# Score and value steps of an attention and MLP kernel gathered into three visits per batch

## The chip, the cores and the metric

The kernel runs on one core of one Trainium2 chip. The metric is the device time of one execution in microseconds (us); the time of the kernel before is the median of three runs. All durations in this document are in us where no other unit stands.

## The reference

Two operators follow each other. The first is causal attention with a window of 64 positions, for 8 batches, 8 heads, 576 positions and a head dimension of 64. The second is a layer norm without bias and an MLP with a ReLU and a residual, on the attention's output with the heads side by side (512 features, 2048 hidden).

```python
scores = scale * np.matmul(q, k.transpose(0, 1, 3, 2))
rel = pos[:, None] - pos[None, :]
mask = (rel >= 0) & (rel < window)                 # window = 64
attn = softmax(np.where(mask, scores, -1e9))
x = np.matmul(attn, v)                             # heads side by side: (8, 576, 512)
xn = (x - mu) / np.sqrt(var + 1e-06) * g_ln
out = x + np.maximum(xn @ w_ch1, 0.0) @ w_ch2      # (512, 2048), (2048, 512)
```

## The kernel before

Work is cut into nine groups. Group g from 0 to 7 is the first 512 positions of batch g; group 8 is the last 64 positions of all eight batches, as four blocks ("tails", one for two batches each). A group has four blocks of 128 rows.

The attention of one block has two steps on TensorE. The score step `s_mm(g, j)` makes 16 small matmuls (64 rows deep, 64 columns wide) into two PSUM banks of the pool `ps_s` (tag "sc"), lets ScalarE take the exp of both banks into an f16 tile `pt`, and `s_mask` multiplies `pt` with the window mask on VectorE. The value step `b_step(g, kb)` makes 16 matmuls (128 deep, 64 stationary columns) of `pt` with the values into the two banks of `ps_x` (tag "xps"); then VectorE makes the rows of the block: reciprocal of the sums, multiplication, mean and variance. `z_step` normalizes these rows on GpSimd, and `zt_step` transposes them, for batches from 2 on by a DMA from SP's queue (block 3 of batches 3 and 5 on TensorE). So the score matmuls, the value matmuls and the full 128x128 matmuls of the MLP are three kinds that use the array in different shapes.

The MLP of a group is a list of units. From group 2 on there are 30: 16 units `l1(hc)`, four matmuls of 512 columns each and a ReLU on ScalarE, with two PSUM banks in turn; then 14 units `stage(n, p)`, two for each of the seven products of a Strassen-like second layer, in the order 1, 2, 6, 5, 7, 4, 3. Three banks A, B and C collect these products. Between products VectorE adds a bank to the residual rows (`post`, line 485), while later products go on accumulating into the same bank: bank A is read after product 1 and then written by product 6. `s_sums` makes sums of the hidden activations on VectorE that the products need.

The MLP of group g and the attention of batch b = g + 1 run together. The order on every engine is written out by hand: `at(i, f, ...)` puts a call into slot i, and after unit i the calls of slot i are made, in the order in which they were put there. The instructions of one engine run in the order of these calls, and the framework puts semaphore waits where a tile is read or reused. Each tile tag has a fixed number of buffers: `ps_s` has two banks, "xps" one tile of two banks, `ps_t` the banks t0 and t1 (for transposes on TensorE and for bank C), `pt` four buffers.

In groups 2 to 6 the value step of block j and the score step of block j+1 share slots 2, 7 and 12; the value step of block 3 stands in slot 17, and the score step of block 0 of the batch after next in slot 27 of the group before (slot 31 of group 1 for batch 3):

```python
            for j in range(4):
                if j:
                    at((2, 7, 12)[j - 1], s_mm, b, j)
                    at((3, 8, 13)[j - 1], s_mask, b, j)
                at((2, 7, 12, 17)[j], b_step, b, j)
                at((2, 7, 12, 17)[j], z_step, b, j)
```

Groups 3 and 5 also carry one tail block each, with its score step in slot 1 and its value step in slot 5. Group 2 carries in addition four `w2_sums` on VectorE (slots 4 to 7). For batches from 4 on, GpSimd casts q and k to f16 in four casts (`cast_qk`, line 128), three in slot 11 and one in slot 16; the q halves are then transposed by DMAs from SP's queue (slot 13) and the k halves on TensorE (slots 17 and 21; 18 and 22 in group 2). The loads of q and k are issued at the end of the group before.

Of the kernel before, what the change touches and what calls it, by code (L numbers as in the profile page):

```python
# [10 lines left out]
FP32 = mybir.dt.float32  # L11
# [4 lines left out]
ALU = mybir.AluOpType  # L16
# [4 lines left out]
def kernel(  # L21
# [10 lines left out]
    nc = tc.nc  # L32
    B, H, S, D = q.shape
# [3 lines left out]
    NGRP = B + 1  # L37
    NKC = DM // 128
    NHC = HID // 128
    NHP = H // 2  # L40
    EPS = 1e-6
    XQ = 3
# [13 lines left out]
    ps_s = ctx.enter_context(tc.tile_pool(name="pss", bufs=2, space=PSUM))  # L56
    ps_x = ctx.enter_context(tc.tile_pool(name="psx", bufs=1, space=PSUM))
# [22 lines left out]
    tail32, tail16, tailT, vT = {}, {}, {}, {}  # L80
# [157 lines left out]
    def t_tail(i, x):  # L238
# [19 lines left out]
        evac(0, tailT[i][x], tp)  # L258

    def s_mm(g, j, pe_mask=False):  # L260
        sc = [ps_s.tile([128, NHP, 2, 64], FP32, tag="sc", name=f"sc_{g}_{j}_{par}") for par in range(2)]
        pt = p_pt.tile([128, 2, NHP, 2, 64], FP16, tag="pt", name=f"pt_{g}_{j}")
        pts[(g, j)] = pt
        if pe_mask:
            m = mbias[:, :]
            mb = bass.AP(tensor=m.tensor, offset=m.offset, ap=[m.ap[0], [0, NHP * 2], m.ap[1]])
            for par in range(2):
                nc.tensor.matmul(
                    out=sc[par][:, :].rearrange("p h w i -> p (h w) i"), lhsT=ident16, rhs=mb,
                    start=True, stop=False, skip_group_check=True,  # L270
                )
# [16 lines left out]

        for par in range(2):
            o, i = pt[:, par], sc[par][:, :]  # L290
            if XQ <= g < NGRP - 1:
                o = o.rearrange("p h w (r j) -> p (h w) r j", j=4)
                i = i.rearrange("p h w (j r) -> p (h w) r j", j=4)
            nc.scalar.activation(out=o, in_=i, func=AF.Exp, bias=0.0, scale=scale)  # L294
# [7 lines left out]

    def b_step(g, kb):
        kblk = f"{g}_{kb}"
        sfx, nb = ("r", 2) if g == NGRP - 1 else ("", None)
# [5 lines left out]
        xn = xv.rearrange("p (h d) -> p h d", h=H)  # L311
        xps = ps_x.tile([128, H, 128], FP32, tag="xps", name=f"xps_{kblk}")
        pt = pts.pop((g, kb))
        for h in range(H):
            par, hp = h % 2, h // 2
            for r in range(2):
                if sfx:
                    rhs = vT[kb][:, r, h, :]
                else:
                    rhs = (vA if r else vB)[g][:, kb, h, :]  # L320
                nc.tensor.matmul(out=xps[64 * r:64 * r + 64, h, :D + 1], lhsT=pt[:, par, hp, r, :], rhs=rhs,  # L321
                                 start=True, stop=True)
        rcp = p_blk.tile([128, H], FP32, tag="rcp", name=f"rcp_{kblk}")
        nc.vector.reciprocal(out=rcp, in_=xps[:, :, D])  # L324
        rcp_b = bass.AP(tensor=rcp.tensor, offset=rcp[:, :].offset,
                        ap=[rcp[:, :].ap[0], rcp[:, :].ap[1], [0, D]])
        nc.vector.tensor_tensor(out=xn, in0=xps[:, :, 0:D], in1=rcp_b, op=ALU.mult)  # L327
        stats = p_blk.tile([128, nc.vector.BN_STATS_DIM], FP32, tag="stats", name=f"stats_{kblk}")
# [512 lines left out]
    for g in range(NGRP):  # L841
# [7 lines left out]
        def at(i, f, *a):  # L849
            slots[min(i, len(slots) - 1)].append((f, a))  # L850

        b = g + 1
        if g == 0:
# [29 lines left out]
        if g == 1:  # L883
# [35 lines left out]
            at(17, make_vB, 3)  # L919
            at(31, s_mm, 3, 0)  # L920
            at(31, s_mask, 3, 0)
            for i, (x, half) in zip((12, 24, 12, 28), ((0, 0), (1, 0), (0, 1), (1, 1))):
# [8 lines left out]
        if g > 1 and g + 2 < B:  # L931
            at(11, alloc_qkT, g + 2)
            if g + 2 >= XQ:
                at(11, cast_qk, g + 2, 0, (0,))
                at(11, cast_qk, g + 2, 1, (0,))
                at(11, cast_qk, g + 2, 0, (1,))
            else:
                at(11, cast_qk, g + 2, 0)
        if g > 1 and b < B:
            for j in range(4):  # L940
                if j:
                    at((2, 7, 12)[j - 1], s_mm, b, j)
                    at((3, 8, 13)[j - 1], s_mask, b, j)
                at((2, 7, 12, 17)[j], b_step, b, j)
                at((2, 7, 12, 17)[j], z_step, b, j)
                at((12, 12, 18, {3: 24, 5: 23}.get(b, 22))[j], zt_step, b, j)
        for n, i in enumerate(TAILS.get(g, ())):
            ts = (13, 13, 17, 22) if n else (1, 2, 5, 11)
            at(ts[0], s_mm, NGRP - 1, i)
            at(ts[1], s_mask, NGRP - 1, i)  # L950
            at(ts[2], b_step, NGRP - 1, i)
            at(ts[2], z_step, NGRP - 1, i)
            at(ts[3], zt_step, NGRP - 1, i)
        n = g + 2
        if g > 1 and n < B:
            at(16, cast_qk, n, 1, (1,) if n >= XQ else (0, 1))
            at(20, alloc_v, n)
# [4 lines left out]
            for i, (x, half) in zip((13, 18, 13, 22) if g == 2 else (13, 17, 13, 21),  # L962
                                    ((0, 0), (1, 0), (0, 1), (1, 1))):
                at(i, t_main, n, x, half, 0)
            at(27, s_mm, n, 0)
            at(28, s_mask, n, 0)
            if n + 1 < B:
# [64 lines left out]
```

## Time and profile before

| what | value |
|---|---|
| runs of the kernel before | 310.21, 308.94, 310.77; median 310.21 us |
| profiled execution, span from first to last instruction | 305.9 us |
| profiled execution, own time | not given beside the span |
| TensorE, share of the span | 97% (295.4 us) |
| VectorE, GpSimd, ScalarE | 72%, 57%, 49% |
| granted clock of TensorE, mean | 0.995 of full speed |
| groups 2, 3, 4, 5, 6, length on TensorE | 31.37, 31.30, 31.36, 31.29, 29.04 us |

In the rows of a timeline the first number is the start in us from the beginning of the span and the second the duration in us; then come the engine, the line of the kernel, the operation, the tile written and the tiles read, the shapes, and the number of instructions merged into the row. In square brackets stands the idle time of the engine before the row and what ended it. Matmuls are pipelined, so a duration contains latency, and the time that a matmul takes up is read from start to start. PE is TensorE, DVE VectorE, ACT ScalarE, POOL GpSimd, SP the queue that issues most DMAs.

Groups start (first `hps` matmul) at 92.50 (group 2), 123.87 (3), 155.17 (4), 186.53 (5), 217.82 (6) and 246.86 (7).

### The profile page before, as it was taken

How to read it: one execution, taken by the hardware profiler on the slowest of the kernel's cores; microseconds unless marked ns; L12 is line 12 of the kernel's file. 1: busy time of each engine (PE TensorE's matmuls, PEld its weight loads, DVE VectorE, ACT ScalarE, POOL GpSimd, SP SyncE). 2: the span in 40 equal slices, each digit the busy share in tenths (PEclk: the TensorE clock that was granted, in tenths of full speed). 3: DMA queues.
4: the chain of work that ended last, by engine and by line, in shares of the span. 5: the costliest groups of instructions: out<-in, count | busy, mean ns of one | idle time of the engine just before them, and what ended most of it. 6: DMA issues, size and time to landing. Idle time of an engine off the chain costs nothing.

```text
span 305.9 us, 7582 instructions
## 1 busy us (share of the span) xinstructions
PE 295.4 (97%) x3061; PEld 196.4 (64%) x3061; DVE 220.6 (72%) x412; ACT 150.7 (49%) x253; POOL 173.3 (57%) x256
## 2 busy tenths in 40 slices
PE   6989999999999999999999999999999999999992
PEld 4557545687454478547854786469646854788882
DVE  0778696767766995589656965896669685789972
ACT  2586635587227733775157527752475046306500
POOL 7589676564952789179806983698146507014300
PEclk9999999999999999999999999999999999999998
DMA  8999999999776997899189997993790399003014
GB/s 191 266 385 301 314 366 286 303 284 236 150 181 228 243 172 147 280 280 127 35 243 303 204 160 245 298 155 70 215 175 19 53 189 208 19 17 139 0 38 103
DMA packets 113669, 58.35 MB, mean 191 GB/s; under 512 B 83617, under 2 KB 104609, under 8 KB 113634
## 3 DMA queue, kind: packets, MB, share of 16 engines
q1 hardware_dynamic: 112576, 54.67, 74.0%
q0 software_dynamic: 768, 2.80, 3.8%
q8 instruction: 24, 0.39, 0.5%
q10 hardware_dynamic: 290, 0.40, 0.5%
q14 instruction: 11, 0.09, 0.1%
HBM read 38.80 MB, written 9.44 MB: 158 GB/s over the span
## 4 chain that ended last, share of the span: by engine, by line
PE 89%; SPq 4%; DMA 2%; POOL 1%; ACT 1%; DVE 1%; issue 0%; ACTq 0%
PE hps L401 30%; PE pA L478 12%; PE pB L478 8%; PE pC L478 8%; PE hph L537 6%; PE ch L413 6%; PE xps L321 4%; PE sc L286 4%; PE ch L554 3%; PE tp L229 3%; PE lA L592 2%; DMA w1s<-in_moe_w_ch_dram 2%; SPq L141 2%; POOL w1g L190 1%; SPq L89 1%; PE lC L592 1%
## 5 line engine op out<-in xcount | busy, mean ns | idle before, releaser
L401 PE MATMUL hps<-zT,w1g 128*128 128x512 f16 x416 | 95.3, 380 | 0.0
L405 ACT ACTIVATE hrT<-hps 128x512 f16<-128x512 f32 x104 | 62.3, 599 | 39.3 <-PE hps L401 35.7
L401 PEld LDWEIGHTS <-w1g 128*128 128x128 f16 x416 | 38.6, 98 | 43.3 <-issue 0.7
L294 ACT ACTIVATE pt<-sc 128x512 f16<-128x512 f32 x72 | 39.0, 594 | 27.7 <-PE sc L286 20.5
L478 PEld LDWEIGHTS <-sS 128*128 128x128 f16 x448 | 43.4, 98 | 4.9
L351 POOL TENSOR_SCALAR rsz<-mvg 128x1 f32<-128x1 f32 x28 | 10.2, 364 | 60.6 <-DVE mvg L332 59.8
L128 POOL CAST qk<-qk 128x1024 f16<-128x1024 f32 x32 | 36.3, 1147 | 11.3 <-DMA qk<-in_k_dram 5.6
L478 PEld LDWEIGHTS <-hrT 128*128 128x128 f16 x336 | 32.4, 98 | 5.5 <-ACT hrT L637 0.3
L301 DVE TENSOR_TENSOR pt<-pt,mask 128x1024 f16<-128x1024 f16 x32 | 27.5, 867 | 8.4 <-ACT pt L294 8.4
L215 ACT COPY qkT<-tp 128x1024 f16<-128x1024 f16 x16 | 16.1, 1012 | 34.1 <-PE tp L229 34.1
L485 DVE TENSOR_TENSOR xn<-pA,xn 128x512 f32<-128x512 f32 x28 | 19.2, 685 | 16.7 <-PE pA L478 11.1
L478 PE MATMUL pC<-w2s,sS 128*128 128x256 f16 x224 | 27.1, 273 | 0.0
L478 PE MATMUL pA<-wT,sS 128*128 128x256 f16 x224 | 26.9, 273 | 0.0
L354 POOL TENSOR_SCALAR z<-xn,rsz 128x512 f16<-128x512 f32 x28 | 24.9, 888 | 2.9
L327 DVE TENSOR_TENSOR xn<-xps,rcp 128x512 f32<-128x512 f32 x36 | 24.9, 691 | 1.5 <-DMA out_dram<-xn 0.3
L329 DVE BATCH_NORM_STATS2 stats<-xn 128x6 f32<-128x512 f32 x36 | 25.0, 695 | 1.2
L324 DVE RECIPROCAL rcp<-xps 128x8 f32<-128x8 f32 x36 | 7.3, 204 | 24.7 <-PE xps L321 24.7
L452 DVE TENSOR_TENSOR sS<-hrT 128x512 f16<-128x512 f16 (+1 forms) x40 | 24.5, 613 | 0.6 <-ACT hrT L405 0.6
L537 PE MATMUL hph<-zT,w1g 128*128 128x256 f16 x192 | 23.8, 273 | 1.0 <-DVE zT L371 0.5
L321 PEld LDWEIGHTS <-pt 128*64 128x64 f16 x576 | 12.2, 110 | 13.7 <-issue 5.5
L352 POOL TENSOR_TENSOR rsz<-rsz,mhalf 128x1 f32<-128x1 f32 x28 | 19.4, 692 | 2.3
L147 POOL CAST vA<-v 128x1024 f16<-128x1024 f32 (+2 forms) x19 | 17.4, 930 | 5.6 <-DMA v<-in_v_dram 5.6
(113 smaller groups left out, 448.9 us busy)
## 6 DMA issues: line engine op xcount, KB each, us to landing
out_dram<-xn SPq DMA_DIRECT2D x33, 256.0 KB, 2.8
qk<-in_q_dram SPq DMA_DIRECT2D x16, 512.0 KB, 6.2
qk<-in_k_dram SPq DMA_DIRECT2D x16, 512.0 KB, 6.9
v<-in_v_dram SPq DMA_DIRECT2D x32, 256.0 KB, 7.7
w2s<-in_moe_w_ch_dram SPq DMA_DIRECT2D x9, 512.0 KB, 9.2
w1s<-in_moe_w_ch_dram SPq DMA_DIRECT2D x4, 512.0 KB, 7.3
tk<-in_k_dram SPq DMA_DIRECT2D x8, 256.0 KB, 4.5
tv<-in_v_dram SPq DMA_DIRECT2D x8, 256.0 KB, 5.0
```

Of the source, the lines that this page charges most:

```text
L128: nc.gpsimd.tensor_copy(out=dst[:, :].rearrange("p (a j) e d -> p a e j d", j=j), in_=t[:, :].rearrange("p (a e j d) -> p a e j d", e=2, j ...
L294: nc.scalar.activation(out=o, in_=i, func=AF.Exp, bias=0.0, scale=scale)
L301: nc.vector.tensor_tensor(out=ptv, in0=ptv, in1=mb, op=ALU.mult)
L321: nc.tensor.matmul(out=xps[64 * r:64 * r + 64, h, :D + 1], lhsT=pt[:, par, hp, r, :], rhs=rhs, start=True, stop=True)
L327: nc.vector.tensor_tensor(out=xn, in0=xps[:, :, 0:D], in1=rcp_b, op=ALU.mult)
L329: nc.vector.bn_stats(out=stats, in_=xv)
L354: nc.gpsimd.tensor_scalar(out=z, in0=xv, scalar1=rs, scalar2=nm, op0=ALU.mult, op1=ALU.add)
L401: nc.tensor.matmul(out=hps, lhsT=w1g[:, kc, 128 * hc:128 * (hc + 1)], rhs=zT[g][:, kc, :], start=(kc == 0), stop=(kc == NKC - 1),)
L405: nc.scalar.activation(out=hrT[:, hc, :], in_=hps, func=AF.Relu, bias=0.0, scale=1.0)
L452: nc.vector.tensor_tensor(out=o, in0=x, in1=y, op=op)
L478: nc.tensor.matmul(out=o, lhsT=a[:, c, 128 * p:128 * p + 128], rhs=wv[:, c, :], start=(first and (p == 0 or split_c) and c == 0), stop=(c ...
L537: nc.tensor.matmul(out=hps[:, e], lhsT=w1g[:, kc, 128 * hc:128 * (hc + 1)], rhs=zT[g][:, kc, 256 * half:256 * half + 256], start=(kc == 0) ...
```

## The change

`s_mm` is split into its matmuls (`s_pe`) and its exps (`s_exp`), and `b_step` into its matmuls (`b_pe`) and its work on VectorE (`b_rows`). Both matmul halves take a parameter `home`, so that scores can also be put into "xps" or into t0 and t1, and values into "sc" or t0 and t1. Where values lie in two tiles, `b_rows` makes two reciprocals and two multiplications of half the size.

In groups 2 to 6 the slots become these. The score steps of blocks 0 and 1 stand together in slot 27 of the group before (slot 30 of group 1), the second with its exps and masks one slot later. Slot 2 has the value step of block 0 and two score steps: blocks 2 and 3, or block 2 and the tail where the group has one. The second one's exps are put into slots 4 and 5, one each, and its mask into slot 5. Slot 7 has the value steps of blocks 1, 2 and 3; in groups 3 and 5 it has those of block 1 and of the tail and the score step of block 3, and slot 12 has the value steps of blocks 2 and 3. The rows of blocks 1, 2 and 3 are made in slots 7, 12 and 17, those of the tail in slot 8. The rows of block 3 come behind the add of bank A that stands in unit 17.

On GpSimd three of the casts of q and k move from slot 11 to slot 5, and the fourth from slot 16 to slot 11. The z transpose of block 1 moves from slot 12 to slot 14. Group 7 keeps its order.

```diff
@@ -257,8 +257,21 @@
                     nc.tensor.transpose(out=tp[:, r, hp, :], in_=src[:, r, 2 * hp:2 * hp + 2, :], identity=ident16)
         evac(0, tailT[i][x], tp)
 
+    scs = {}
+
     def s_mm(g, j, pe_mask=False):
-        sc = [ps_s.tile([128, NHP, 2, 64], FP32, tag="sc", name=f"sc_{g}_{j}_{par}") for par in range(2)]
+        s_pe(g, j, pe_mask)
+        s_exp(g, j, 0, 1)
+
+    def s_pe(g, j, pe_mask=False, home="sc"):
+        if home == "xps":
+            both = ps_x.tile([128, 2, NHP, 2, 64], FP32, tag="xps", name=f"sc_{g}_{j}")
+            sc = [both[:, par] for par in range(2)]
+        elif home == "t":
+            sc = [ps_t.tile([128, NHP, 2, 64], FP32, tag=f"t{par}", name=f"sc_{g}_{j}_{par}") for par in range(2)]
+        else:
+            sc = [ps_s.tile([128, NHP, 2, 64], FP32, tag="sc", name=f"sc_{g}_{j}_{par}") for par in range(2)]
+        scs[(g, j)] = sc
         pt = p_pt.tile([128, 2, NHP, 2, 64], FP16, tag="pt", name=f"pt_{g}_{j}")
         pts[(g, j)] = pt
         if pe_mask:
@@ -266,7 +279,7 @@
             mb = bass.AP(tensor=m.tensor, offset=m.offset, ap=[m.ap[0], [0, NHP * 2], m.ap[1]])
             for par in range(2):
                 nc.tensor.matmul(
-                    out=sc[par][:, :].rearrange("p h w i -> p (h w) i"), lhsT=ident16, rhs=mb,
+                    out=sc[par][:, :, :, :].rearrange("p h w i -> p (h w) i"), lhsT=ident16, rhs=mb,
                     start=True, stop=False, skip_group_check=True,
                 )
         for hp in range(NHP):
@@ -286,8 +299,10 @@
                     nc.tensor.matmul(out=sc[par][:, hp, iw, :], lhsT=lhsT, rhs=rhs,
                                      start=not pe_mask, stop=True, skip_group_check=pe_mask)
 
-        for par in range(2):
-            o, i = pt[:, par], sc[par][:, :]
+    def s_exp(g, j, *pars):
+        pt, sc = pts[(g, j)], scs[(g, j)]
+        for par in pars:
+            o, i = pt[:, par], sc[par][:, :, :, :]
             if XQ <= g < NGRP - 1:
                 o = o.rearrange("p h w (r j) -> p (h w) r j", j=4)
                 i = i.rearrange("p h w (j r) -> p (h w) r j", j=4)
@@ -301,6 +316,34 @@
         nc.vector.tensor_tensor(out=ptv, in0=ptv, in1=mb, op=ALU.mult)
 
     def b_step(g, kb):
+        b_pe(g, kb)
+        b_rows(g, kb)
+
+    xpss = {}
+
+    def b_pe(g, kb, home="xps"):
+        kblk = f"{g}_{kb}"
+        tail = g == NGRP - 1
+        if home == "xps":
+            tiles = [ps_x.tile([128, H, 128], FP32, tag="xps", name=f"xps_{kblk}")]
+        elif home == "t":
+            tiles = [ps_t.tile([128, H // 2, 128], FP32, tag=f"t{i}", name=f"xps_{kblk}_{i}") for i in range(2)]
+        else:
+            tiles = [ps_s.tile([128, H // 2, 128], FP32, tag="sc", name=f"xps_{kblk}_{i}") for i in range(2)]
+        xpss[(g, kb)] = tiles
+        n = H // len(tiles)
+        pt = pts.pop((g, kb))
+        for h in range(H):
+            par, hp = h % 2, h // 2
+            for r in range(2):
+                if tail:
+                    rhs = vT[kb][:, r, h, :]
+                else:
+                    rhs = (vA if r else vB)[g][:, kb, h, :]
+                nc.tensor.matmul(out=tiles[h // n][64 * r:64 * r + 64, h % n, :D + 1], lhsT=pt[:, par, hp, r, :],
+                                 rhs=rhs, start=True, stop=True)
+
+    def b_rows(g, kb):
         kblk = f"{g}_{kb}"
         sfx, nb = ("r", 2) if g == NGRP - 1 else ("", None)
         if kb % 2 == 0:
@@ -309,22 +352,15 @@
                     x_norm[(g, h)] = p_xn.tile([128, 2, DM], FP32, tag="xn" + sfx, name=f"xn_{g}_{h}", bufs=nb)
         xv = x_norm[(g, kb // 2)][:, kb % 2, :]
         xn = xv.rearrange("p (h d) -> p h d", h=H)
-        xps = ps_x.tile([128, H, 128], FP32, tag="xps", name=f"xps_{kblk}")
-        pt = pts.pop((g, kb))
-        for h in range(H):
-            par, hp = h % 2, h // 2
-            for r in range(2):
-                if sfx:
-                    rhs = vT[kb][:, r, h, :]
-                else:
-                    rhs = (vA if r else vB)[g][:, kb, h, :]
-                nc.tensor.matmul(out=xps[64 * r:64 * r + 64, h, :D + 1], lhsT=pt[:, par, hp, r, :], rhs=rhs,
-                                 start=True, stop=True)
+        tiles = xpss.pop((g, kb))
+        n = H // len(tiles)
         rcp = p_blk.tile([128, H], FP32, tag="rcp", name=f"rcp_{kblk}")
-        nc.vector.reciprocal(out=rcp, in_=xps[:, :, D])
-        rcp_b = bass.AP(tensor=rcp.tensor, offset=rcp[:, :].offset,
-                        ap=[rcp[:, :].ap[0], rcp[:, :].ap[1], [0, D]])
-        nc.vector.tensor_tensor(out=xn, in0=xps[:, :, 0:D], in1=rcp_b, op=ALU.mult)
+        for i, xps in enumerate(tiles):
+            nc.vector.reciprocal(out=rcp[:, n * i:n * i + n], in_=xps[:, :, D])
+        for i, xps in enumerate(tiles):
+            rc = rcp[:, n * i:n * i + n]
+            rcp_b = bass.AP(tensor=rc.tensor, offset=rc.offset, ap=[rc.ap[0], rc.ap[1], [0, D]])
+            nc.vector.tensor_tensor(out=xn[:, n * i:n * i + n], in0=xps[:, :, 0:D], in1=rcp_b, op=ALU.mult)
         stats = p_blk.tile([128, nc.vector.BN_STATS_DIM], FP32, tag="stats", name=f"stats_{kblk}")
         nc.vector.bn_stats(out=stats, in_=xv)
         if g not in mvg:
@@ -848,6 +884,14 @@
 
         def at(i, f, *a):
             slots[min(i, len(slots) - 1)].append((f, a))
+
+        def first_scores(b, i):
+            at(i, s_pe, b, 0)
+            at(i, s_pe, b, 1, False, "xps")
+            at(i, s_exp, b, 0, 0, 1)
+            at(i + 1, s_exp, b, 1, 0, 1)
+            at(i + 1, s_mask, b, 0)
+            at(i + 2, s_mask, b, 1)
 
         b = g + 1
         if g == 0:
@@ -917,8 +961,7 @@
             at(14, cast_v, 3, 2, 4)
             at(17, alloc_vB, 3)
             at(17, make_vB, 3)
-            at(31, s_mm, 3, 0)
-            at(31, s_mask, 3, 0)
+            first_scores(3, 30)
             for i, (x, half) in zip((12, 24, 12, 28), ((0, 0), (1, 0), (0, 1), (1, 1))):
                 at(i, t_main, 3, x, half, 0)
             at(40, load_qk, 4, 0)
@@ -929,22 +972,52 @@
                 at(4 + 2 * m, w2_sums, i, 0, 4)
                 at(5 + 2 * m, w2_sums, i, 4, 8)
         if g > 1 and g + 2 < B:
-            at(11, alloc_qkT, g + 2)
-            if g + 2 >= XQ:
-                at(11, cast_qk, g + 2, 0, (0,))
-                at(11, cast_qk, g + 2, 1, (0,))
-                at(11, cast_qk, g + 2, 0, (1,))
+            at(5, alloc_qkT, g + 2)
+            at(5, cast_qk, g + 2, 0)
+            at(5, cast_qk, g + 2, 1, (0,))
+            at(11, cast_qk, g + 2, 1, (1,))
+        if g > 1 and b < B:
+            tail = TAILS.get(g)
+            at(2, b_pe, b, 0)
+            at(2, b_rows, b, 0)
+            at(2, z_step, b, 0)
+            at(2, s_pe, b, 2)
+            at(2, s_exp, b, 2, 0, 1)
+            at(3, s_mask, b, 2)
+            if tail:
+                r, i = NGRP - 1, tail[0]
+                at(2, s_pe, r, i, False, "t")
+                at(4, s_exp, r, i, 0)
+                at(5, s_exp, r, i, 1)
+                at(5, s_mask, r, i)
+                at(7, b_pe, b, 1)
+                at(7, b_pe, r, i, "t")
+                at(7, s_mm, b, 3)
+                at(7, b_rows, b, 1)
+                at(7, z_step, b, 1)
+                at(8, s_mask, b, 3)
+                at(8, b_rows, r, i)
+                at(9, z_step, r, i)
+                at(12, b_pe, b, 2)
+                at(12, b_pe, b, 3, "sc")
+                at(16, zt_step, r, i)
             else:
-                at(11, cast_qk, g + 2, 0)
-        if g > 1 and b < B:
+                at(2, s_pe, b, 3, False, "t")
+                at(4, s_exp, b, 3, 0)
+                at(5, s_exp, b, 3, 1)
+                at(5, s_mask, b, 3)
+                at(7, b_pe, b, 1)
+                at(7, b_pe, b, 2, "t")
+                at(7, b_pe, b, 3, "sc")
+                at(7, b_rows, b, 1)
+                at(7, z_step, b, 1)
+            at(12, b_rows, b, 2)
+            at(12, z_step, b, 2)
+            at(17, b_rows, b, 3)
+            at(17, z_step, b, 3)
             for j in range(4):
-                if j:
-                    at((2, 7, 12)[j - 1], s_mm, b, j)
-                    at((3, 8, 13)[j - 1], s_mask, b, j)
-                at((2, 7, 12, 17)[j], b_step, b, j)
-                at((2, 7, 12, 17)[j], z_step, b, j)
-                at((12, 12, 18, {3: 24, 5: 23}.get(b, 22))[j], zt_step, b, j)
-        for n, i in enumerate(TAILS.get(g, ())):
+                at((12, 14, 18, {3: 24, 5: 23}.get(b, 22))[j], zt_step, b, j)
+        for n, i in enumerate(TAILS.get(g, ()) if b >= B else ()):
             ts = (13, 13, 17, 22) if n else (1, 2, 5, 11)
             at(ts[0], s_mm, NGRP - 1, i)
             at(ts[1], s_mask, NGRP - 1, i)
@@ -953,7 +1026,6 @@
             at(ts[3], zt_step, NGRP - 1, i)
         n = g + 2
         if g > 1 and n < B:
-            at(16, cast_qk, n, 1, (1,) if n >= XQ else (0, 1))
             at(20, alloc_v, n)
             at(20, cast_v, n, 0, 2)
             at(21, cast_v, n, 2, 4)
@@ -962,8 +1034,7 @@
             for i, (x, half) in zip((13, 18, 13, 22) if g == 2 else (13, 17, 13, 21),
                                     ((0, 0), (1, 0), (0, 1), (1, 1))):
                 at(i, t_main, n, x, half, 0)
-            at(27, s_mm, n, 0)
-            at(28, s_mask, n, 0)
+            first_scores(n, 27)
             if n + 1 < B:
                 at(40, load_qk, n + 1, 0)
                 at(40, load_qk, n + 1, 1)
```

## The prediction

> **What bounds the kernel now.** I read the page first, then the waits, then TensorE's timeline, then the other engines' timelines group by group. The page says that TensorE is the bound:
>
> ```profile
> PE 295.4 (97%) x3061; PEld 196.4 (64%) x3061; DVE 220.6 (72%) x412; ACT 150.7 (49%) x253; POOL 173.3 (57%) x256
> ```
>
> The waits give TensorE no wait of weight in groups 2 to 7. So an edit can gain only by shortening what TensorE issues, and loses wherever it makes TensorE wait. TensorE's timeline of group 4 (start, duration, both in us) shows what could be shortened:
>
> ```profile
> 157.89 0.22 PE L321 MATMUL xps<-vB,pt 128*64 128x65 f16 x1
> ...
> 158.11 0.19 PE L321 MATMUL xps<-vB,pt 128*64 128x65 f16 x1
> ...
> 158.14 0.19 PE L321 MATMUL xps<-vB,pt 128*64 128x65 f16 x1
> ...
> 158.27 0.41 PE L286 MATMUL sc<-qkT,qkT 64*128 64x64 f16 x16
> 158.61 4.49 PE L401 MATMUL hps<-zT,w1g 128*128 128x512 f16 x20
> 163.03 0.22 PE L321 MATMUL xps<-vB,pt 128*64 128x65 f16 x1
> ```
>
> Each change of matmul kind costs about 0.11 us. Four MLP matmuls take 0.863 (0.216 each), so the 20 at 158.61 need 4.32, but the next step starts 4.42 later: 0.10 for MLP to value, the first half of that kind. Pairs of value matmuls start 0.033 apart, so 16 take 0.27, yet the score step starts 0.38 after the value step: 0.11. Sixteen score matmuls start within 0.22 of each other (0.41 less one duration of 0.19), so they need 0.23, yet the MLP resumes 0.34 after them: 0.11.
>
> ScalarE has almost no room. Between visits a ReLU starts every 0.86:
>
> ```profile
> 159.68 0.60 ACT L405 ACTIVATE hrT<-hps 128x512 f16<-128x512 f32 x1
> 160.54 0.60 ACT L405 ACTIVATE hrT<-hps 128x512 f16<-128x512 f32 x1 [0.26 <-PE hps L401]
> ```
>
> It starts 1.06 after the first matmul of its unit and ends at 1.66; the unit that reuses the bank starts at 1.73. An exp queued between takes 0.49. The row below is such a case in group 7, where exps stand between ReLUs: 16 matmuls need 3.46 plus 0.10, and took 3.70 (249.02 to 252.72). So 0.14 was lost.
>
> ```profile
> 249.02 3.77 PE L401 MATMUL hps<-zT,w1g 128*128 128x512 f16 x16
> 252.72 0.45 PE L321 MATMUL xps<-vt,pt 128*64 128x65 f16 x16
> ```
>
> VectorE has a deadline. Product 6 accumulates into bank A, so it may not start before `post("A", 0, 0)` has read that bank. Group 3 (start 123.87), first VectorE, then GpSimd and TensorE:
>
> ```profile
> 133.15 0.21 DVE L324 RECIPROCAL rcp<-xps 128x8 f32<-128x8 f32 x1 [0.33 <-PE xps L321]
> 134.95 0.66 DVE L301 TENSOR_TENSOR pt<-pt,mask 128x1024 f16<-128x1024 f16 x1
> 140.08 1.46 DVE L301 TENSOR_TENSOR pt<-pt,mask 128x1024 f16<-128x1024 f16 x1
> 141.46 1.25 DVE L452 TENSOR_TENSOR sS<-hrT 128x512 f16<-128x512 f16 x1
> 144.56 0.68 DVE L485 TENSOR_TENSOR xn<-pA,xn 128x512 f32<-128x512 f32 x1
> 138.98 3.46 POOL L128 CAST qk<-qk 128x1024 f16<-128x1024 f32 x3
> 145.55 1.91 PE L478 MATMUL pA<-wT,sS 128*128 128x256 f16 x16
> ```
>
> From 133.15 VectorE runs almost without a gap; its add ends at 145.24, product 6 starts at 145.55: 0.31 of slack. And the f16 operations that meet GpSimd's casts wait: the mask takes 1.46 instead of 0.66, a sum 1.25 instead of 0.42, together 1.63.
>
> **The change part by part.** Times are from the start of a group ("T").
>
> *Fewer kind changes: gain.* Before, a batch costs 3+3+3+2 changes in slots 2, 7, 12, 17, and a tail batch four more. After, groups 2, 4, 6 have 3 (slot 2: b0, s2, s3) + 2 (slot 7: b1, b2, b3) = 5 of 11. Groups 3 and 5 have 3 (b0, s2, tail score) + 3 (b1, tail value, s3) + 2 (b2, b3) = 8 of 15. The visit with s0 keeps 2 and takes s1 along. Removed: 3x6 + 2x7 = 32, at 0.108 each 3.46 us. No place in the trace puts two steps of one kind side by side; such a boundary costs from 0 to 0.11. I take 0, since inside a step every matmul already changes weights and PSUM address at the 0.033 pitch. [...]
>
> *Exps of the second score step in slots 4 and 5: loss.* The first sits between ReLU 4 and ReLU 5: 0.49 + 0.49 against a period of 0.86 makes ReLU 5 late by 0.11, less the slack of about 0.02: 0.09 on unit 7. The second falls before the visit in slot 7, which hides it. Bounds 0 and 0.14 (the group 7 row); 5 groups x 0.09 = 0.45.
>
> *Masks in time for slot 7: nothing.* The last exp ends at T+7.66, the mask at about T+8.4; its value step stands second (tail, T+8.47) or third (T+8.74). If a q cast gets in first, the mask waits about 0.9.
>
> *The adds for bank A, tail groups 3 and 5: loss.* Product 6 was due at T+21.68; it moves up by 7 changes (0.77) and by s1's 0.23, and back by 0.09: T+20.77. VectorE's run begins with the rows of block 1, at T+8.69 instead of T+9.28, because the visit in slot 7 is earlier. Its length was 12.09 (133.15 to 145.24). Out go one mask, 0.58, the 0.15 of waiting for block 2, and the 1.63 of waiting on casts. In come the tail's rows, which were in an idle stretch around slot 5 before: 1.80 from reciprocal to mask at 133.15, about 1.95 with the two half tiles (one more reciprocal, two half multiplies). Casts now start after GpSimd's z of block 0, about T+8.2; three in a row at about 1.02 last to T+11.3, so the mask of block 3, queued at T+10.5, waits 0.87; the fourth (behind z of block 1 and of the tail, about T+17.5) costs 0.28. New length 12.83, end T+21.5, late by 0.75. Bounds: no cast met (0) and all of 1.63 met (1.25). 2 x 0.75 = 1.5.
>
> *The same in group 2: loss.* The four `w2_sums` keep slots 4 to 7; two now stand behind the mask of block 3, in the cast train. Each waits one cast, so the rows of block 1 start at T+11.6, not T+8.36. The rest: 1.80 rows, 2.61 sums, 1.95 rows, 2.26 sums, 0.68 add = 9.30, end T+20.9, against product 6 at T+19.97 (20.76 less 0.65, less 0.23, plus 0.09). Loss 0.9; bounds 0 (at most one cast met) and 2.0.
>
> *Groups 4 and 6: nothing.* Rows at T+8.7 plus 9.30 is T+18.0, with one cast met T+19.0, due T+19.96.
>
> *Casts earlier, q transposes and z: nothing.* Casts in slot 5 now wait in GpSimd's queue for their loads (6.2 and 6.9 us to landing, issued from T+1.5 to T+2.6 on), with z of block 1 queued behind. On SP the two q transposes stand between z transposes 0 and 1. Nothing that TensorE reads before slot 17 depends on it, and the zT are needed only at T+31. If that cover went, each cast would cost 1.0. z of block 3, the v casts and the two vB copies follow the rows of block 3; in tail groups they move about 0.1 to 0.3 back. The last copy is issued at 152.47, lands by the median of its kind 4.1 later, and the value step that reads it starts at 157.89: 1.3 spare, so nothing; bounds 0 and 0.5.
>
> *Banks: nothing.* Block 3's values stay in the sc banks until its rows behind bank A's add (to about T+23); s0 wants them at slot 27. Block 2's leave t0 and t1 before the transposes of slot 17; xps is free when s1 takes it.
>
> Sum: -3.46 + 0.45 + 1.5 + 0.9 = -0.6 us. The profiled execution has a span of 305.9; no separate time is given for it, and the median of the runs is 310.21 (308.94 to 310.77), so 4.3 us lie around the span and stay. **Forecast: 305.3 of span, 309.6 us.** A measurement of this kernel tells about 0.5% (1.55 us) from no change.
>
> [...]
>
> **The rivals.**
>
> *B, VectorE keeps pace.* The casts fall beside rows, which read PSUM and were not slowed in the trace (0.69 beside casts and away from them), and the deadline holds. Then -3.46 + 0.45 = -3.0, 307.2. For it: the casts move by a few tenths and my margins are that small. Against it: the added 1.95 of rows stands whatever the casts do, and the deadline is 0.9 earlier.
>
> *C, the casts hold VectorE up everywhere; slower.* Place: the f16 operations between slot 5 and bank A's add in groups 2 to 5. Price by the trace's wait per cast, 0.82: four casts in group 2, 9.30 + 1.2 + 3.3 from T+8.45 is T+22.2, 2.3 late; tail groups 1.3 each; three casts in group 4, T+20.5, 0.5 late. Sum 5.4 + 0.45 - 3.46 = +2.4, 312.6. It decides once the waits exceed 3.0 in sum. Against it: a rows step of 1.8 can hide one or two casts.
>
> *D, the change doesn't shorten as it says.* If boundaries within a kind cost 0.11 too, 20 of them (5 + 9 + 6) give back 2.2: +1.6, 311.8. The 0.033 pitch speaks against it.
>
> **How the numbers follow.** Forecast 0.54, with its own range 308.2 to 311.2: 0.12 of it is below 308.66 and 0.42 within 0.5%. B 0.26, C 0.15, D 0.05. Faster 0.12 + 0.26 = 0.38; same 0.42; slower 0.20. The range takes in B's 307.2 and most of C: 307.0 to 312.0.
>
> **What would show it.** Right: 32 fewer kind changes; a ReLU about 0.1 late in slot 5; a wait of TensorE for VectorE's add on bank A before product 6 in groups 2, 3 and 5 of 0.5 to 1.2 each and none in 4 and 6; the masks done before slot 7. Wrong: no such waits (B), waits in group 4 too (C), or value steps that begin 0.38 apart (D).

## The result and the profile after

The changed kernel took 308.98 us (median of 22 runs, 306.33 to 315.63); 22 runs of the kernel before, taken with them, had a median of 309.52 (308.55 to 312.39). The ratio is 0.9952, 95% interval 0.9929 to 0.9975. This ratio leaves out runs more than 1.5% above the fastest run of their kernel, here six of the 22 after; over all runs the medians differ by only 0.17%. The forecast was 309.6 in a range of 307.0 to 312.0. The profiled execution after took 306.33 with a span of 304.6 (before: 305.9).

TensorE is still the bound; its line of the page:

```profile
PE 293.3 (96%) x3061; PEld 196.4 (64%) x3061; DVE 218.4 (72%) x432; ACT 150.5 (49%) x253; POOL 169.1 (56%) x256
```

The lengths of the groups on TensorE, from the first MLP matmul of one to that of the next:

| kernel | group 2 | 3 | 4 | 5 | 6 | sum |
|---|---|---|---|---|---|---|
| before | 31.37 | 31.30 | 31.35 | 31.30 | 29.04 | 154.36 |
| after | 31.45 | 30.88 | 30.82 | 30.94 | 28.23 | 152.33 |

So 2.03 less, of which 0.23 is the score step of batch 3's block 1, now done in group 1. The net gain is 1.8. Group 2 starts 0.74 later (93.24 for 92.50): that 0.23, and 0.5 of start-up that differs from run to run (group 2 starts between 92.5 and 94.7 in the thirteen profiles of this case). From the start of group 7's MLP to the end it is 59.0 in both.

The visits, in TensorE's timeline of group 4 after (start, duration):

```profile
158.29 0.22 PE L343 MATMUL xps<-vB,pt 128*64 128x65 f16 x1
...
158.67 0.64 PE L299 MATMUL sc<-qkT,qkT 64*128 64x64 f16 x32
159.25 4.59 PE L437 MATMUL hps<-zT,w1g 128*128 128x512 f16 x20
163.76 0.22 PE L343 MATMUL xps<-vB,pt 128*64 128x65 f16 x1
...
164.54 0.20 PE L343 MATMUL xps<-vA,pt 128*64 128x65 f16 x1
164.66 1.04 PE L437 MATMUL hps<-zT,w1g 128*128 128x512 f16 x4
```

Two score steps are one row of 32, and the MLP resumes 0.58 after its start: twice 0.23 and one change of 0.11. The three value steps from 163.76 to 164.54 are 48 matmuls, 0.78 for 47 distances: 0.0166 each, the pitch inside one step. The boundaries between these steps of one kind cost nothing: the pitch is the same across them. The 20 MLP matmuls now take 4.51 up to the value step, where they took 4.42.

The last is ScalarE's doing; its timeline in the same place:

```profile
161.18 0.60 ACT L441 ACTIVATE hrT<-hps 128x512 f16<-128x512 f32 x1 [0.27 <-PE hps L437]
161.68 0.59 ACT L309 ACTIVATE pt<-sc 128x512 f16<-128x512 f32 x1
162.15 0.60 ACT L441 ACTIVATE hrT<-hps 128x512 f16<-128x512 f32 x1
```

The second ReLU starts 0.97 after the first, not 0.86; unit 7 then starts 0.10 late, in all five groups.

Bank A's deadline in group 3 (start 124.70): VectorE, then GpSimd, then TensorE.

```profile
133.38 0.21 DVE L359 RECIPROCAL rcp<-xps 128x8 f32<-128x8 f32 x1 [0.28 <-PE xps L343]
...
135.17 1.33 DVE L316 TENSOR_TENSOR pt<-pt,mask 128x1024 f16<-128x1024 f16 x1
136.42 0.24 DVE L359 RECIPROCAL rcp<-xps 128x4 f32<-128x4 f32 x2
...
138.25 0.71 DVE L488 TENSOR_TENSOR sS<-hrT 128x1024 f16<-128x1024 f16 x1
...
142.59 0.55 DVE L488 TENSOR_TENSOR sS<-hrT 128x512 f16<-128x512 f16 x1
...
144.98 0.68 DVE L521 TENSOR_TENSOR xn<-pA,xn 128x512 f32<-128x512 f32 x1
```

```profile
132.49 3.48 POOL L128 CAST qk<-qk 128x1024 f16<-128x1024 f32 x3
...
141.82 1.04 POOL L128 CAST qk<-qk 128x1024 f16<-128x1024 f32 x1
```

```profile
143.73 1.91 PE L514 MATMUL pB<-w2s,hrT 128*128 128x256 f16 x16
145.72 1.03 PE L514 MATMUL pA<-wT,sS 128*128 128x256 f16 x8
```

(A row at the end of the stretch asked for counts only what lay in it: product 6 has 16 matmuls, of which the row shows 8.) The mask meets the casts (1.33 for 0.66), the tail's rows run from 136.42 to 138.25, the first half-size sum loses 0.13 to the fourth cast, and the add ends at 145.66. Sixteen matmuls of this step take 1.75, so product 6 could have started at 145.48 and waits 0.24. It waits 0.31 in group 5 and 0.51 in group 2, and not at all in groups 4 and 6.

One wait was not forecast. GpSimd's timeline in group 4 (start 155.58), then SP's:

```profile
176.20 0.19 POOL L387 TENSOR_SCALAR rsz<-mvg 128x1 f32<-128x1 f32 x1 [2.03 <-DVE mvg L368]
...
177.12 0.26 POOL L389 TENSOR_SCALAR rsz<-mvg,rsz 128x1 f32<-128x1 f32 x1
178.76 0.76 POOL L390 TENSOR_SCALAR z<-xn,rsz 128x512 f16<-128x512 f32 x1 [1.37 <-DMA zT<-z]
```

```profile
167.61 1.89 SPq L106 DMA_DIRECT2D tq<-in_q_dram  x1
...
173.39 0.90 SPq L108 DMA_DIRECT2D tv<-in_v_dram  x1
174.45 1.84 SPq L398 DMA_TRANSPOSE zT<-z  x1
```

`z` has three buffers; z of block 3 reuses that of block 0 and must wait until block 0's transpose has read it. That transpose stands on SP behind the six loads of the tails and landed at 178.59. Block 3 of this batch is transposed on TensorE (`ztp`), which therefore started at 179.57, 0.11 late.

### The profile page after: what moved, and what is told of

It reads as the page before. It is cut to its first block, busy times and chain, and to the rows that moved or that the text cites. A ratio compares the mean times of both kernels' runs of the same rounds, so it can differ in the third digit from the quotient of the medians.

```text
span 304.6 us, 7598 instructions
## 1 busy us (share of the span) xinstructions
PE 293.3 (96%) x3061; PEld 196.4 (64%) x3061; DVE 218.4 (72%) x432; ACT 150.5 (49%) x253; POOL 169.1 (56%) x256
## 4 chain that ended last, share of the span: by engine, by line
PE 75%; DVE 12%; SPq 3%; ACT 3%; POOL 2%; issue 2%; DMA 1%; POOLq 0%; ACTq 0%
PE hps L437 21%; PE pA L514 9%; PE pC L514 8%; PE hph L573 6%; PE pB L514 6%; PE ch L449 6%; DVE sS L488 4%; PE ch L590 3%; PE sc L299 3%; PE xps L343 3%; PE tp L229 3%; SPq L141 2%; PE lA L628 2%; DVE xn L363 2%; ACT pt L309 2%; DVE stats L365 2%
## 5 line engine op out<-in xcount | busy, mean ns | idle before, releaser
L437 PEld LDWEIGHTS <-w1g 128*128 128x128 f16 x416 | 39.2, 98 | 45.4 <-issue 2.2
L316 DVE TENSOR_TENSOR pt<-pt,mask 128x1024 f16<-128x1024 f16 x32 | 24.8, 779 | 17.9 <-ACT pt L309 17.9
L363 DVE TENSOR_TENSOR xn<-xps,rcp 128x512 f32<-128x512 f32 (+1 forms) x46 | 25.5, 573 | 1.2 <-DMA out_dram<-xn 0.3
L390 POOL TENSOR_SCALAR z<-xn,rsz 128x512 f16<-128x512 f32 x28 | 23.1, 826 | 4.2 <-DMA zT<-z 1.4
L488 DVE TENSOR_TENSOR sS<-hrT 128x512 f16<-128x512 f16 (+1 forms) x40 | 23.1, 577 | 1.1 <-ACT hrT L441 1.1
L573 PEld LDWEIGHTS <-w1g 128*128 128x128 f16 x192 | 17.9, 98 | 3.0 <-DVE zT L407 0.7
L449 PE MATMUL ch<-w2s,hrT 128*128 128x512 f16 x80 | 19.3, 380 | 0.0
```

The source lines that it names most:

```text
L316: nc.vector.tensor_tensor(out=ptv, in0=ptv, in1=mb, op=ALU.mult)
L363: nc.vector.tensor_tensor(out=xn[:, n * i:n * i + n], in0=xps[:, :, 0:D], in1=rcp_b, op=ALU.mult)
L390: nc.gpsimd.tensor_scalar(out=z, in0=xv, scalar1=rs, scalar2=nm, op0=ALU.mult, op1=ALU.add)
L437: nc.tensor.matmul(out=hps, lhsT=w1g[:, kc, 128 * hc:128 * (hc + 1)], rhs=zT[g][:, kc, :], start=(kc == 0), stop=(kc == NKC - 1),)
L449: nc.tensor.matmul(out=ch[kb], lhsT=hrT[:, hc, 128 * kb:128 * (kb + 1)], rhs=w2s[:, hc, :], start=(hc == 0), stop=(hc == NHC - 1),)
L488: nc.vector.tensor_tensor(out=o, in0=x, in1=y, op=op)
```

## Experiments

**The same kernel again (e0_after).** No edit.

> The kernel after, unchanged, timed beside its variants. Theory: groups 2 to 6 together are 1.9 to 2.1 shorter than in the kernel before (0.2 of it is the score step that moved to group 1), unless GpSimd's z of block 3 waits for a z transpose (1.4 us of such waits in the first profile of after, none in the one of before); then up to 2.3 less. The start, up to group 2, differs from run to run by up to 2. Ratio 0.993 to 0.998.

Six runs: 306.24, 307.36, 310.99, 311.33, 311.64 and 312.07, median 311.16, against 309.56 for 23 runs of before. The ratio, 0.9897 (0.9853 to 0.9941), comes from 306.24 and 307.36 alone. The profile is of the 312.07 run, and shows what made this run long: group 4 takes 35.14, the others as above (31.45, 30.89, 30.89, 28.23). In it, GpSimd and then TensorE:

```profile
182.91 0.76 POOL L390 TENSOR_SCALAR z<-xn,rsz 128x512 f16<-128x512 f32 x1 [3.42 <-DMA zT<-z]
```

```profile
183.73 0.61 PE L402 MATMUL ztp<-ident,z 128*128 128x128 f16 x4 [2.64 <-POOL z L390]
184.13 3.38 PE L514 MATMUL pA<-wT,sS 128*128 128x256 f16 x16
```

The transposes wait 2.8 in all, and the 16 matmuls behind them last 3.38 where they took 1.91. The windows of the trace (stretch, length, busy times, and third from the end the granted clock of TensorE) give the reason:

```profile
180.00:183.70 3.70, 1.09 (x10) 0.73 (x8) 0.06 (x1) 0.39 (x1) 0.79 (x3) 1.00 1.41 145
183.70:187.20 3.50, 3.47 (x19) 2.60 (x20) 0.00 (x0) 0.59 (x1) 3.50 (x6) 0.51 0.58 117
```

For 3.4 us after the gap TensorE had half its clock: some 1.6 more. GpSimd's wait is the same as in the first profile, 1.4 there and 3.4 here. The expectation allowed such waits up to 2.3; group 4 lost 4.3, of which 2.7 is the longer wait and 1.6 the clock.

**A fourth buffer for z (e8_z4).** The order of the instructions is untouched; a constant moves into a free buffer to make room.

```diff
-        z = p_blk.tile([128, DM], FP16, tag="z", name=f"z_{g}_{kb}")
+        z = p_blk.tile([128, DM], FP16, tag="z", name=f"z_{g}_{kb}", bufs=4)
...
-    g1 = p_const.tile([1, DM], FP32, tag="g1", name="g1")
+    g1 = p_in.tile([1, DM], FP32, tag="tq32", name="g1", bufs=1)
```

> The kernel after with four buffers for z in place of three (the 2 KB for it come from g1, which shares a tail buffer; the order of the instructions is the same on every engine). Theory: with three buffers z of block 3 in groups 2, 4 and 6 writes the buffer that the transpose of z of block 0 reads, and that transpose is issued behind the tail loads; with four it has no such wait, so GpSimd's waits for zT are 0 (1.4 after; 2.4 and 3.5 in two variants), TensorE's wait before the transposes of z in group 4 (0.11 after, 2.26 in the variant with split sums) is at most 0.1, and the median is 0.1 to 0.8 below that of the kernel after, with fewer runs over 309. Rival (the landing of that transpose never reaches TensorE in the kernel after): same times as after within 0.1.

308.03 (307.27 to 310.15, 12 runs), ratio 0.9949 (0.9923 to 0.9974). The wait for the transpose is gone, z of block 3 starts 21.9 after the start of its group instead of 23.2, and `ztp` isn't late. The median is 3.1 below the six runs of the changed kernel on the same chip and 0.95 below its first 22 runs, where 0.1 to 0.8 was expected; the ratio is that of the changed kernel.

**The loads of the tails later (e11_tail_loads_later).** The other way to take the wait away: three buffers, but block 0's transpose ahead of the loads on SP.

```diff
-                at(1, load_tail, i)
+                at(13, load_tail, i)
```

> The kernel after with three z buffers as it has, and the first tail loads of groups 2, 4 and 6 moved from slot 1 to slot 13, so that on SP's queue they stand behind the z transpose of block 0 and the q transposes. Theory (z of block 3 waits because that transpose is issued behind six tail loads): it is issued about 4 earlier (about T+14 in group 4, not T+19 to T+20.5) and lands before T+18, so GpSimd waits for no z transpose, TensorE waits at most 0.1 before the transposes of z in group 4, and no run is lengthened by 2 to 5: median 0.5 to 1.5 below that of the kernel after, as with four buffers. The tail's casts in slot 24 may then wait for their loads (0 to 0.6 on the transposes of the tail's q). Rival (the landing is late because the DMA queues are full there, whatever the order): waits for z transposes of 1 or more stay.

307.9 (306.67 to 310.5, 12 runs), ratio 0.9957 (0.9927 to 0.9986). SP in group 4 (start 155.93):

```profile
169.35 1.41 SPq L398 DMA_TRANSPOSE zT<-z  x1
170.85 2.64 SPq L223 DMA_TRANSPOSE qkT<-qk  x2
173.54 0.63 SPq L106 DMA_DIRECT2D tq<-in_q_dram  x1
```

Block 0's transpose landed 16.9 after the start of the group instead of 23.0, and neither GpSimd nor `ztp` waits. Block 2's transpose was issued 1.1 earlier than in the changed kernel but landed later, 30.87 after the start instead of 29.1, and group 5's MLP waits 0.30 for it, so group 4 is 31.01. That the moved loads delay it is not shown: with four buffers and the loads in their old place it landed at 30.75.

Two different cures of one wait both end the long runs: of the changed kernel 10 of 28 runs lie above 310.9, of the four versions in whose profiles z does not wait (these two and the two at the end) 1 of 42, of the kernel before 6 of 82. On the one chip where the changed kernel and e8_z4 ran side by side it is 4 of 6 against 0 of 12.

**The second pair of `w2_sums` later (e1_w2_late).** Out of the cast train, from slots 6 and 7 to 21, behind bank A's add.

```diff
-                at(4 + 2 * m, w2_sums, i, 0, 4)
-                at(5 + 2 * m, w2_sums, i, 4, 8)
+                at((4, 21)[m], w2_sums, i, 0, 4)
+                at((5, 21)[m], w2_sums, i, 4, 8)
```

> The kernel after, with the last two of the four w2_sums of group 2 moved from slots 6 and 7 to slot 21, where VectorE sits idle. Theory (32 kind changes less ReLU delays less waits for bank A's add): in group 2 the w2_sums met the casts (2.96 for two of them instead of 1.28) and pushed the rows of block 1 back by 2.4. Without them these rows begin at about T+8.7 and the wait before product 6 of group 2 goes from 0.51 to 0; groups 3 and 5 keep theirs (0.24 and 0.31), and group 2 is shorter by about 0.5. Rival (product 6 waits for something else than VectorE's queue): the wait of group 2 stays at 0.4 to 0.6.

The wait of 0.51 before product 6 in group 2 is gone, but the group still takes 31.42 (one run, 307.67): z now waits for the transpose of block 0 in group 2 too and then takes 1.65 beside the moved sums, so the tail's q cast behind it starts 28.32 after the start of the group, as it did without the edit (28.35), and the transposes of tail q, which are due 0.5 earlier, wait for it. The two rows, GpSimd and TensorE:

```profile
117.72 1.65 POOL L390 TENSOR_SCALAR z<-xn,rsz 128x512 f16<-128x512 f32 x1 [1.14 <-DMA zT<-z]
```

```profile
123.66 0.40 PE L248 MATMUL tpq<-ident,tq 128*128 128x128 f16 x4 [0.55 <-POOL tq L118]
```

So the 0.51 was real, and another wait stood behind it. With four buffers the same edit brings 0.65 (below).

**Sums split in the tail groups (e2_split_sums).** In groups 3 and 5 half of the first sums goes to slot 4, ahead of the casts' conflict.

```diff
-                at(7 + i, s_sums, 0, 4, i)
+                if g in (3, 5):
+                    at(4, s_sums, 0, 2, i)
+                    at(7 + i, s_sums, 2, 4, i)
+                else:
+                    at(7 + i, s_sums, 0, 4, i)
```

> The kernel after, with the first half of the sums of the hidden activations in groups 3 and 5 split in two: chunks 0 and 1 in slot 4, in VectorE's idle 2.0 between the masks of slot 3 and slot 5, chunks 2 and 3 where all four stood. Theory: VectorE's run from the rows of block 1 to bank A's add gets shorter by about 1.1 (2.55 for four sums becomes about 1.45), so the waits of 0.24 and 0.31 before product 6 of groups 3 and 5 go to 0, with group 2 unchanged at about 0.5; GpSimd's z of block 0 and the casts behind it move back by 0 to 1. Rival (the tail's value step or the casts hold product 6, whatever VectorE has to do): the waits stay within 0.1.

The waits before product 6 in groups 3 and 5 are gone, the tail's value step waits 0.14 for its mask in return, and both groups take 30.82 (30.88 and 30.94). Group 4 took 32.97, with a wait of 2.26 at `ztp`: the transpose landed 25.2 after the start of the group. One run of 309.68 shows nothing on the time, then. The edit also has a price that was not expected: from the start of group 7 to the end it takes 59.26 instead of 59.03, which is more than the 0.18 that groups 3 and 5 gain. All three versions with split sums show it and no other; why is open.

**Casts back to their old slots (e3_casts_old), and the casts alone moved (e4_casts_alone).** The first is the changed kernel with

```diff
-            at(5, alloc_qkT, g + 2)
-            at(5, cast_qk, g + 2, 0)
-            at(5, cast_qk, g + 2, 1, (0,))
-            at(11, cast_qk, g + 2, 1, (1,))
+            at(11, alloc_qkT, g + 2)
+            at(11, cast_qk, g + 2, 0)
+            at(11, cast_qk, g + 2, 1, (0,))
+            at(16, cast_qk, g + 2, 1, (1,))
```

and the second the kernel before with the changed kernel's slots for them.

> The kernel after with the four casts of q and k put back into slots 11 (three) and 16 (one). Theory: the casts then run behind z of block 1 (and of the tail), from about T+14 to T+18, and meet the sums of slots 13 to 15 instead of the mask of block 3; the wait before product 6 becomes 0.5 to 2.0 in groups 3 and 5, about 0 to 0.8 in group 4, 0 to 0.5 in group 2; and the q transposes land later, where the score steps of slot 27 now start about 0.9 earlier than in the kernel before, which had 0.12 to spare in group 4, so these wait 0.5 to 1.5 in some of the groups 2 to 5. Together 2 to 8 us slower than the kernel after. Rival (the cast move is a side matter): within 0.7 us of the kernel after.

> The kernel before with only the casts of q and k moved (three to slot 5, one to slot 11). Theory (the gain is in the kind changes): TensorE has no new wait, the mask of block 3 and the sum behind it no longer wait for casts, TensorE's groups keep their lengths within 0.1 each; the time is within 0.7 us of the kernel before. Rival (the cast move carries the gain): faster than before by 1 to 2 us.

The old slots under the new visits: 309.93, ratio 1.0014 (0.9981 to 1.0047), groups 31.59, 32.02, 30.87, 32.03, 28.23. The casts now meet the half-size sums, and bank A's add ends 22.1 after the start of group 3, not 21.0. VectorE and TensorE in group 3 (start 125.72):

```profile
143.79 1.14 DVE L488 TENSOR_TENSOR sS<-sS,hrT 128x512 f16<-128x512 f16 x1
144.85 1.25 DVE L488 TENSOR_TENSOR sS<-hrT 128x512 f16<-128x512 f16 x1
...
147.15 0.68 DVE L521 TENSOR_TENSOR xn<-pA,xn 128x512 f32<-128x512 f32 x1
```

```profile
144.71 0.62 PE L229 MATMUL tp<-ident,qk 128*128 128x128 f16 x8 [0.24 <-POOL qk L128]
...
147.89 1.36 PE L514 MATMUL pA<-wT,sS 128*128 128x256 f16 x11 [0.81 <-DVE xn L521]
```

Product 6 waits 0.97 and k's transposes 0.41 in groups 3 and 5. The score steps of slot 27 do not wait, against my expectation. The groups together are 2.4 longer than in the changed kernel, at the lower end of the 2 to 8 expected. The new slots under the old visits: 309.5, ratio 1.0003 (0.9975 to 1.0032), groups 31.69, 31.31, 31.27, 31.30, 29.03, with tail q's transposes 0.33 late in group 2. So neither half gains alone: the visits need the earlier casts to meet the earlier deadline, and the casts bring nothing where there was slack.

**One score step a slot later (e5_s3_apart).** It adds back two changes of kind in groups 2, 4 and 6, and nothing else.

```diff
-                at(2, s_pe, b, 3, False, "t")
+                at(3, s_pe, b, 3, False, "t")
```

> The kernel after with the score step of block 3 in groups 2, 4 and 6 taken out of slot 2 and put into slot 3: two more kind changes in each of these groups, the same matmuls. Theory: each change costs 0.108, so groups 2, 4 and 6 get longer by 0.22 each (0.65 in all), unless another wait hides it in group 2. Rival (what the change gained is not the kind changes): these groups stay within 0.05.

Group 6 is 0.22 longer, which is twice 0.108; group 2 is 0.18 longer, with 0.05 less to wait before product 6. Group 4 is 2.86 longer, of which 2.65 is the wait at `ztp` (2.76 for 0.11); the rest is 0.21. The one run took 309.48.

**Both exps in slot 4 (e6_exps_together).**

```diff
-                at(4, s_exp, b, 3, 0)
-                at(5, s_exp, b, 3, 1)
+                at(4, s_exp, b, 3, 0, 1)
```

(and the same for the tail).

> The kernel after with both exps of the second score step of slot 2 put into slot 4, none in slot 5. Theory: two exps of 0.49 between ReLU 4 and ReLU 5 make ReLU 5 late by 0.60 in place of 0.11, so TensorE waits 0.58 before unit 7 in place of 0.10 in each of groups 2 to 6; where product 6 waits for bank A's add (groups 2, 3 and 5) part of it is given back there, in groups 4 and 6 none: 0.48 longer each. Rival (the 0.10 before unit 7 is not ScalarE's): the wait stays 0.10.

Unit 7 waits 0.59 in all five groups. The waits before product 6 vanish, since TensorE now comes later to them. Groups: 31.30, 31.12, 31.19, 31.12, 28.72, in sum 1.1 more than after. The one run took 307.75.

**Four buffers, late `w2_sums` and split sums together (e9_all); the v casts earlier as well (e10_v).** The first is the edits of e8_z4, e1_w2_late and e2_split_sums in one; the second adds

```diff
-            at(20, cast_v, n, 0, 2)
-            at(21, cast_v, n, 2, 4)
+            at(16, cast_v, n, 0, 2)
+            at(16, cast_v, n, 2, 4)
```

> Four z buffers, the last two w2_sums of group 2 in slot 21, and the first half of the sums in groups 3 and 5 split (chunks 0 and 1 in slot 4). Theory: no wait before product 6 (0.51, 0.24, 0.31 after), no wait on zT, and a small one (0.15) of the tail's value step in slot 7 for its mask; group 2 shorter by 0.4 to 0.5 than after, groups 3 and 5 by 0.06 to 0.2, group 4 by 0 to 0.1; 0.7 in all, ratio to before about 0.992 to 0.995. Rival (the wait of group 2 passes on to the transposes of the tail's q, as in the variant with the w2_sums alone, 0.62 there, because GpSimd's queue is full and not because z waits): group 2 no shorter than 31.40.

> As the one with all three, and the casts of v moved from slots 20 and 21 to slot 16, ahead of z of block 3, into a stretch of 1.9 in which GpSimd waits for VectorE. Theory: the tail's q cast comes 2 earlier, so the transposes of the tail's q no longer wait in group 2 (0.14 after): group 2 shorter by another 0.1; the sums before bank A's add may meet one cast (0.3 to 0.8), which the slack of groups 2 to 6 holds in part: the time within 0.5 of the kernel with all three.

The first took **306.81** (306.07 to 308.26, 6 runs), ratio 0.9902 (0.9872 to 0.9932), the lowest median of this case. Groups: 30.80, 30.82, 30.78, 30.82, 28.23, 0.88 less than after, and product 6 follows product 2 without a wait (TensorE, group 3):

```profile
143.81 1.80 PE L514 MATMUL pB<-w2s,hrT 128*128 128x256 f16 x15
145.45 1.91 PE L514 MATMUL pA<-wT,sS 128*128 128x256 f16 x16
```

Group 2 gains the 0.65 that e1_w2_late could not show. Of the 0.88, 0.25 is lost again near the end, where a wait in the last group's first layer grows from 0.07 to 0.30, as in e2_split_sums. The second took 307.96 (306.98 to 311.88, 12 runs), ratio 0.9957 (0.9929 to 0.9985): group 2 is 31.37, with two new waits of 0.28 each in the products that collect in banks B and C. The expected 0.1 of gain there was wrong, and the median is 1.15 above the kernel with all three, where at most 0.5 was expected.

## Why the prediction was right, point by point, and where it was not

**Fewer kind changes: right.** 32 at 0.108. The check is group 4, which has the change without a wait of VectorE: 6 x 0.108 = 0.65 less, 0.10 back for the ReLU and 0.11 back at `ztp` make -0.44, and the 0.07 that tail q's transposes waited before is gone too: -0.51. Measured: -0.53. Rival D is refuted by the 0.0166 pitch across two boundaries, and e5_s3_apart has the price from the other side.

**Exps in slots 4 and 5: right.** 0.10 on unit 7, forecast 0.09; 5 x 0.10 = 0.50. With both exps together 0.59.

**Waits before product 6: in the right groups, too large.** Forecast 0.9, 0.75 and 0.75 in groups 2, 3 and 5; measured 0.51, 0.24 and 0.31, so 1.06 for 2.4, and two of the three lie below the 0.5 to 1.2 that was to show it right. In group 3 product 6 was due 20.78 after the start (forecast 20.77) and VectorE's run began at 8.68 (forecast 8.69); the mis-sized term is the run's length, 12.28 and not 12.83. The mask lost 0.67 to the casts, not 0.87; the tail's rows took 1.83, not 1.95; the fourth cast cost 0.13, not 0.28: 0.47 of the 0.55. In group 2 two `w2_sums` took 2.96 where two of that size took 1.28 before the train, the rows began at 11.35 (forecast 11.6), and the add ended at 20.51 (forecast 20.9). Rival B, no such waits, did not come, nor did C, waits in group 4. But a wait of C's kind shows in e3_casts_old, where two of the half-size sums meet a cast each: 0.97 late in each tail group (C said 1.3, with more casts met).

The f16 operations on VectorE that began during a cast took longer, as in the trace before (1.46 for 0.66, 1.25 for 0.42): in group 3 after, the mask took 1.33 for 0.66, and in e3_casts_old two sums took 1.14 and 1.25 for 0.42. The mask ends 0.53 after the three casts (136.50, 135.97) and the second of the sums 0.27 after them (146.10, 145.83). What makes them wait is not shown.

**"Casts earlier, q transposes and z: nothing": wrong, and this is what failed.** The step asked when TensorE reads the transposes and what would come later; it did not ask what comes earlier, and when the buffer of z is free for it. In group 4 VectorE's run to bank A's add has no mask left in it and loses 0.7 to casts where it lost 1.6, so the add ends 18.7 after the start of the group, where it ended at 20.4. The rows of block 3 follow that add in both kernels, so GpSimd reaches z of block 3 at 21.8, where it was at 23.6 before. The two rows in group 4 before (start 155.17), VectorE and GpSimd:

```profile
174.93 0.68 DVE L485 TENSOR_TENSOR xn<-pA,xn 128x512 f32<-128x512 f32 x1
```

```profile
178.79 1.01 POOL L354 TENSOR_SCALAR z<-xn,rsz 128x512 f16<-128x512 f32 x1
```

Block 0's transpose landed at 23.4 before, so the trace had only 0.2 of slack on this buffer, and it lands at 22.6 to 25.9 in the profiles of the new order (all but e11_tail_loads_later). `ztp` is due at 23.9, and its z must start 0.8 ahead of that. That is the 0 to 2.8 that group 4 loses from run to run, and e8_z4 and e11_tail_loads_later show it by taking it away in two ways. What makes the landing differ by 3 us between the profiles, and by 2.7 between the two of the changed kernel (it is issued 18.3 to 20.5 after the start of the group, and takes 3.7 to 5.7 from there) is not settled. That all long runs are of this kind is argued, not shown: only one was profiled.

**The sum.** On TensorE's groups: -3.46 + 0.50 + 1.06, and +0.2 for small waits (0.10 more at the start of group 2, 0.11 at `ztp`, 0.05 at tail q's transposes, less the 0.07 of group 4), is -1.7; measured -1.8. The forecast of -0.6 was 1.2 too high, nearly all of it in product 6. The 16 runs of the changed kernel up to 310.9 say the same: their median, 307.77, is 1.75 below that of the kernel before. Over all runs the median moved by only 0.54. That this agrees with the forecast of -0.6 is luck: the waits before product 6 were set 1.3 too high, and the long runs, for which the sum had no term, took about as much away. With the six runs of e0_after the changed kernel has a median of 309.45 over 28 runs, and the kernel before 309.46 over 82, so the median shows no gain.

**The level.** "4.3 us lie around the span" compared one execution with the median of others. Runs with both numbers show 1.7 to 2.4 around the span (306.33 and 304.6, 308.77 and 306.4). The profiled execution of before was a short one: its group 2 starts at 92.5, the earliest of the thirteen profiles.

## What to carry to other kernels

Steps of one kind set side by side saved 0.108 us per change of kind that disappeared, but moving a step up also moves the deadlines of every engine behind it: first the add that frees a bank, then the buffer two engines away. For each moved step list the buffers it reuses and when the last reader of each lands, DMA landings with their spread included. Where an edit that removes a wait brings nothing, look for the next wait before dropping it: the late `w2_sums` gained 0.03 alone and 0.65 with a fourth buffer for z.

## What the runs showed of the hardware

After an idle gap of 2.64 us TensorE ran about 3.4 us at half clock (the profile of e0_after; a granted clock of 0.51 over the 3.50 us shown above, and of 1.00 over the 2.80 us behind them). Gaps of 2.10 us in e2_split_sums and 2.60 us in e5_s3_apart were followed by a clock of 1.00 (183.00 to 187.00 and 180.00 to 187.50), so in these runs a wait of this length cost half as much again, or nothing. What decided between the two is not shown; no run tested it on purpose.
